# Two pieces of a cos/sin table issued on the ACT queue, and all pieces of the input back to back on the SP queue

## Chip, cores and metric

One core of one Trainium2 chip. The metric is the device time of one execution in microseconds (us). "Span" is the time from the first to the last instruction in the trace, about 1.8 us less than the device time.

The names of the engines in what follows: PE multiplies matrices; DVE, ACT and POOL work element by element; SP only issues loads. DMA is the moving of data by 16 engines of its own. A load is first issued by a queue (here that of SP or of ACT), then its packets move, and it has landed when its completion is recorded; only then may an engine that waits for it go on.

## The reference

A pre-norm layer: a spectral filter (2D real FFT, product with a complex weight, inverse FFT) on the layer-normed input, and then a gated feed-forward block.

```python
x = A_x                                              # 1 x 2048 x 576, bf16
h  = x + irfft2(rfft2(layernorm(x)) * (A_w_r + 1j * A_w_i))
h2 = h + (gelu(layernorm(h) @ B_w_gate) * (layernorm(h) @ B_w_up)) @ B_w_down
```

## The kernel before

The change touches only how the first loads are issued. The input x is loaded in five pieces (tiles 0-1, 2-3, 4-7, 8-11, 12-15 of 128 x 576; called x0 to x4), the cos/sin table ATB in three (tiles 0-3, 4-7, 8-15; called table 0, 1, 2). DVE and ACT compute row statistics of x (`bn_stats` on DVE; Identity and Square with a sum on ACT for tiles 1, 3, 7, 11, 13), the table is scaled by 1/std, and PE multiplies x by the scaled table.

```python
def x_load(i, c0, c1):
    P.dma(SP, XO[:, c0:c1, 0:D], xv[:, c0:c1, :], f"x{i}", w=[("X", c) for c in range(c0, c1)])
def atb_load(i, c0, c1):
    P.dma(SP, ATB[:, c0:c1, :], tabs[:, c0:c1, :], f"atb{i}", w=[("ATB", c) for c in range(c0, c1)])
x_load(0, 0, 2)
x_load(1, 2, 4)
atb_load(0, 0, 4)
x_load(2, 4, 8)
atb_load(1, 4, 8)
x_load(3, 8, 12)
x_load(4, 12, 16)
atb_load(2, 8, 16)
# ... cut: FT, BT, VT tables, then 36 loads of the two weight planes w_i, w_r, all on SP ...
P.op(ACT, lambda a: a.activation(SA[:, 0, 0:1], EPT[:, 0:1], ACTF.Sqrt), r=["EPT"], ...)  # dummy: brings the table load early
act_sum(1); act_sq(1)              # ACT: first use of x0
ln1_tile(0); ln1_tile(2)           # DVE: bn_stats of tile 0 (x0) and tile 2 (x1)
# ... cut: act_sum(3), variance, Sqrt, reciprocal ...
ln1_scale(0, DVE)                  # DVE: first use of table 0
# ... cut: groups 1 to 4, the same on x1 .. x4 ...
for i in range(NG):                # POOL: third weight plane = -w_i, 16 instructions
    P.op(POOL, lambda v, g=GORD[i]: v.tensor_scalar(WS[:, g, 0, :], WS[:, g, 2, :], -1.0, None, op0=ALU.mult), ...)
```

The helper makes each engine wait on semaphores for the loads and results that it reads. Each load has a semaphore of its own.

## Time and profile before

| | before |
|---|---|
| device time, median of 3 runs (lowest to highest) | 504.44 us (504.13 to 504.98) |
| span of the profiled run | 502.9 us |
| start of DVE's first instruction on x | 3.84 us |
| first matmul of the next stage (FT) | 20.33 us |

The page of the kernel before: first the line of busy time by engine, then the chain that ended last.

```profile
PE 492.4 (98%) x4318; PEld 297.7 (59%) x4319; DVE 183.9 (37%) x391; ACT 158.7 (32%) x296; POOL 39.1 (8%) x49
...
PE 91%; DVE 6%; issue 1%; DMA 1%; ACT 1%; DVEq 0%
```

PE is the engine to feed, and DMA holds 1% of the chain. That 1% is the landing of x0 (3.1 us). Of the 6% of DVE (30.5 us) 12.9 lie before 20.4 us and 17.3 between 33 and 55 us, behind all of these loads. The pieces of x and of the table are read in the first 20 us, so I read the timeline there. Its columns are start, length, engine, line, operation, written and read tiles, count, and in brackets the idle time before and what ended it. SPq is the issuing of loads by the SP queue.

```profile
0.72 1.28 ACT L517 ACT_TABLE_LOAD   x1 [0.72 <-PEq L907]
0.73 0.87 SPq L206 DMA_DIRECT2D XO<-in_A_x_dram  x2
...
1.30 0.10 POOL L378 MEMSET EPT<- 128x1 f32 x1
...
1.65 0.42 SPq L206 DMA_DIRECT2D ATB<-c_atab  x1
...
2.02 0.20 ACT L517 ACTIVATE SA<-EPT 128x1 f32<-128x1 f32 x1
2.11 0.43 SPq L206 DMA_DIRECT2D XO<-in_A_x_dram  x1
...
2.59 0.43 SPq L206 DMA_DIRECT2D ATB<-c_atab  x1
...
3.06 0.91 SPq L206 DMA_DIRECT2D XO<-in_A_x_dram  x2
...
3.84 1.55 DVE L440 BATCH_NORM_STATS2 ST<-XO 128x6 f32<-128x288 bf16 x4 [3.84 <-DMA XO<-in_A_x_dram]
...
6.44 0.42 DVE L472 TENSOR_SCALAR ATS<-ATB,RS 128x128 bf16<-128x128 bf16 x2
...
8.16 2.25 DVE L440 BATCH_NORM_STATS2 ST<-XO 128x6 f32<-128x288 bf16 x6
...
17.75 8.16 POOL L665 TENSOR_SCALAR WS<-WS 128x290 bf16<-128x290 bf16 x8 [2.05 <-DMA WS<-in_A_w_i_dram]
```

What to see: an issue takes about 0.43 us, one follows the other, and DVE waits for a load once, 3.84 us for x0. That a load is late is no cost by itself; the cost is the wait in brackets.

### The profile page before, as it was taken

The numbers are of one execution on the slowest core, as the hardware profiler recorded it, in microseconds if no ns is written. First come the engines' busy times: TensorE is split into PE (matmuls) and PEld (weight loads), VectorE is DVE, ScalarE is ACT, GpSimd is POOL, SyncE is SP. The second block draws the span as 40 slices with busy tenths as digits, with TensorE's granted clock in tenths as the row PEclk, the third lists the DMA queues.
The fourth block names the chain that finished last, engine by engine and source line by source line (L and its number), as shares of the span: only waits on it lengthen the run. The fifth ranks groups of instructions, "written<-read, shape, count | busy, mean of one in ns | idle before, by whom it ended". The sixth has DMA issues, their size and how long they took to land.

```text
span 502.9 us, 9972 instructions
## 1 busy us (share of the span) xinstructions
PE 492.4 (98%) x4318; PEld 297.7 (59%) x4319; DVE 183.9 (37%) x391; ACT 158.7 (32%) x296; POOL 39.1 (8%) x49
## 2 busy tenths in 40 slices
PE   6899999999999999999999999999999999999998
PEld 2687674444458764444477744444577644444775
DVE  5899673344431114343310134333201233333111
ACT  7888776653220003333200023323100133323000
POOL 3644281000000000000000000000000000000000
PEclk9999999999999999999999999999999999999999
DMA  8779789001100000100000001100000000000000
GB/s 284 165 224 334 235 292 353 6 4 25 25 5 13 18 19 17 22 17 1 2 7 18 19 15 23 22 4 1 1 18 19 13 1 1 1 2 2 12 19 19
DMA packets 25948, 28.64 MB, mean 57 GB/s; under 512 B 11568, under 2 KB 19888, under 8 KB 25776
## 3 DMA queue, kind: packets, MB, share of 16 engines
q1 hardware_dynamic: 23328, 17.39, 12.1%
q0 software_dynamic: 2576, 10.62, 6.3%
q8 instruction: 34, 0.56, 0.5%
q14 instruction: 10, 0.08, 0.1%
HBM read 23.66 MB, written 2.36 MB: 52 GB/s over the span
## 4 chain that ended last, share of the span: by engine, by line
PE 91%; DVE 6%; issue 1%; DMA 1%; ACT 1%; DVEq 0%
PE PS L838 56%; PE PS L861 28%; PE PS L700 3%; DVE TP L629 2%; PE PS L739 2%; PE PS L600 1%; DVE ST L440 1%; DVE CUS L606 1%; PE PS L645 1%; DVE CUS L607 1%; DMA XO<-in_A_x_dram 1%; PE PS L620 1%; DVE U L505 0%; DVE ATS L472 0%; ACT JNK L431 0%
## 5 line engine op out<-in xcount | busy, mean ns | idle before, releaser
L838 PE MATMUL PS<-HT,WGU 64*128 64x512 bf16 x2592 | 281.9, 376 | 0.0
L838 PEld LDWEIGHTS PS<-HT,WGU 64*128 64x128 bf16 x2592 | 137.3, 94 | 143.4 <-issue 1.2
L850 ACT ACTIVATE GL<-PS 128x512 bf16<-128x512 f32 x144 | 85.9, 597 | 289.3 <-PE PS L838 289.3
L851 DVE TENSOR_TENSOR AT<-GL,PS 128x512 bf16<-128x512 bf16 x144 | 99.0, 688 | 174.1 <-PE PS L838 172.5
L861 PE MATMUL PS<-WD,AT 128*128 128x288 bf16 (+2 forms) x1152 | 141.8, 286 | 0.0
L861 PEld LDWEIGHTS PS<-WD,AT 128*128 128x128 bf16 x1152 | 111.0, 98 | 31.5 <-issue 1.7
L864 DVE TENSOR_TENSOR OS<-PS,XO 128x288 bf16<-128x288 f32 (+2 forms) x32 | 14.7, 458 | 125.8 <-PE PS L861 125.8
L665 POOL TENSOR_SCALAR WS<-WS 128x290 bf16<-128x290 bf16 x16 | 15.2, 949 | 9.3 <-DMA WS<-in_A_w_i_dram 8.2
L742 DVE SCALAR_TENSOR_TENSOR XO<-PS,XO 128x576 bf16<-128x576 f32 x16 | 12.1, 756 | 8.4 <-PE PS L739 8.4
L645 PE MATMUL PS<-VT,ZS 128*128 128x256 bf16 x96 | 13.4, 272 | 1.7 <-DVE ZS L631 1.4
L600 PE MATMUL PS<-FT,U 128*128 128x290 bf16 x96 | 14.4, 287 | 0.5 <-DVE U L505 0.5
L700 PE MATMUL PS<-DT,V 128*128 128x289 bf16 x96 | 14.6, 287 | 0.2 <-DVE V L651 0.2
L629 DVE TENSOR_TENSOR TP<-YS,WS 128x580 bf16<-128x580 bf16 (+2 forms) x34 | 13.5, 438 | 0.3 <-issue 0.3
L656 ACT ACTIVATE V<-PS 128x768 bf16<-128x768 f32 x15 | 12.2, 811 | 2.1 <-PE PS L645 1.8
L623 ACT ACTIVATE YS<-PS 128x578 bf16<-128x578 f32 x16 | 10.5, 655 | 3.3 <-PE PS L620 3.3
L494 PE MATMUL PS<-ATS,XO 128*128 128x128 bf16 (+1 forms) x80 | 7.1, 223 | 4.4 <-POOL ATS L467 2.7
L709 ACT ACTIVATE GS<-PS 128x578 bf16<-128x578 f32 x15 | 9.8, 655 | 4.2 <-PE PS L700 4.1
L645 PEld LDWEIGHTS PS<-VT,ZS 128*128 128x128 bf16 x96 | 8.1, 97 | 4.8 <-DVE ZS L631 1.0
L600 PEld LDWEIGHTS PS<-FT,U 128*128 128x128 bf16 x96 | 9.2, 98 | 3.0 <-issue 0.7
L700 PEld LDWEIGHTS PS<-DT,V 128*128 128x128 bf16 x96 | 8.9, 97 | 3.4 <-DVE V L651 0.4
L730 ACT ACTIVATE OS<-XO 128x576 bf16<-128x576 bf16 x16 | 10.8, 675 | 0.0
L620 PE MATMUL PS<-CUS,BT 128*128 128x289 bf16 (+2 forms) x96 | 10.7, 247 | 0.0
(58 smaller groups left out, 158.6 us busy)
## 6 DMA issues: line engine op xcount, KB each, us to landing
WD<-in_B_w_down_dram POOLq DMA_DIRECT2D x9, 576.0 KB, 8.3
WGU<-in_B_w_up_dram SPq DMA_DIRECT2D x4, 1152.0 KB, 9.6
WGU<-in_B_w_gate_dram POOLq DMA_DIRECT2D x4, 1152.0 KB, 10.4
out_dram<-OS SPq DMA_DIRECT2D x30, 72.0 KB, 1.6
XO<-in_A_x_dram SPq DMA_DIRECT2D x3, 576.0 KB, 6.9
IT<-c_itab SPq DMA_DIRECT2D x1, 1024.0 KB, 7.0
HT<-HN SPq DMA_TRANSPOSE x60, 2.4
XO<-in_A_x_dram SPq DMA_DIRECT2D x2, 288.0 KB, 3.2
```

What stands on the lines that cost most here:

```text
L600: P.op(PE, lambda t, b=b, o=o, dt=dt, us=us, g=g: t.matmul(bank(b, 0, 128, 0, 2 * HK), U[:, us, g, :, :], FT[:, o, dt, :], start=(dt == 0) ...
L620: P.op(PE, lambda t, b=b, tb=tb, pl=pl, q0=q0, q1=q1, m=m, s3=s3, sp_=sp_: t.matmul(bank(b, 0, 128, q0, q1), BT[:, sp_, tb, :], CUS[:, s3, ...
L629: P.op(DVE, lambda v, sl=sl, g=g, q0=q0, q1=q1, t_=t_, w_=w_: v.tensor_tensor(TP[:, sl, t_, :, q0:q1], YS[:, sl, :, q0:q1], WS[:, g, w_, q ...
L645: P.op(PE, lambda t, b=b, o=o, c=c, zp=zp, sl=sl, sp_=sp_: t.matmul(bank(b, 0, 128, o, o + 256), ZS[:, sl, zp, 128 * c:128 * c + 128], VT[ ...
L656: P.op(ACT, lambda a, g=g, src=src: a.activation(V[:, :, :, g, :], src, ACTF.Copy), r=[("PS", bs[0]), ("PS", bs[2]), "Vfree"], w=[("V", g, ...
L665: P.op(POOL, lambda v, g=GORD[i]: v.tensor_scalar(WS[:, g, 0, :], WS[:, g, 2, :], -1.0, None, op0=ALU.mult), r=[k for k in wkeys[0 if 1 <= ...
L700: P.op(PE, lambda t, b=b, h=h, i=i, kt=kt, c=c: t.matmul(bank(b, 0, 128, 0, K2), V[:, kt, c, :, :], DT[:, 3 * h + i, 0:K2], start=(i == 0) ...
L838: op = P.op(PE, lambda t, h0=h0, kt=kt, wt=wt, f=f, b=b, HT=HT, s=(half == 0 and j in (0, 5)), e=(half == 1 and j in (3, 8)): t.matmul(ban ...
L850: P.op(ACT, lambda a, s2=s2, b0=b0: a.activation(GL[:, s2, :], bank(b0), ACTF.Gelu_apprx_tanh), r=[("PS", b0)], w=[("GL", s2)])
L851: P.op(DVE, lambda v, s2=s2, b0=b0, f=f: v.tensor_tensor(AT[:, f, :], GL[:, s2, :], bank(b0 + 1), op=ALU.mult), r=[("GL", s2), ("PS", b0 + ...
L861: P.op(PE, lambda t, b=b, d0=d0, d1=d1, f=f, p=p: t.matmul(bank(b, 0, 128, 0, d1 - d0), AT[:, f, 128 * p:128 * p + 128], WD[:, f, d0:d1], ...
L864: P.op(DVE, lambda v, b=b, d0=d0, d1=d1, p=p, c=c: v.tensor_tensor(OS[:, p % 2, d0:d1], bank(b, 0, 128, 0, d1 - d0), XO[:, c, d0:d1], op=A ...
```

## The change

The intent: take the two table pieces off the SP queue, so that x2 is issued one slot earlier and x3, x4 and all later loads two slots earlier, and hide the two issues on ACT, "behind its table load", where ACT waits for x0 anyway.

```diff
-    def atb_load(i, c0, c1):
-        P.dma(SP, ATB[:, c0:c1, :], ...
+    def atb_load(i, c0, c1, eng=SP):
+        P.dma(eng, ATB[:, c0:c1, :], ...
     x_load(0, 0, 2)
     x_load(1, 2, 4)
-    atb_load(0, 0, 4)
     x_load(2, 4, 8)
-    atb_load(1, 4, 8)
     x_load(3, 8, 12)
     x_load(4, 12, 16)
     atb_load(2, 8, 16)
@@
     P.op(ACT, lambda a: a.activation(SA[:, 0, 0:1], EPT[:, 0:1], ACTF.Sqrt), r=["EPT"], w=[("SA0", 0)])
+    atb_load(0, 0, 4, ACT)
+    atb_load(1, 4, 8, ACT)
     idle_mm(11, 0)
```

More of the change, by code (lines that the diff above doesn't have):

```diff
@@ L385, in x_load @@
         P.dma(SP, XO[:, c0:c1, 0:D], xv[:, c0:c1, :], f"x{i}", w=[("X", c) for c in range(c0, c1)])
-    def atb_load(i, c0, c1):
-        P.dma(SP, ATB[:, c0:c1, :], tabs[:, c0:c1, :], f"atb{i}", w=[("ATB", c) for c in range(c0, c1)])
+    def atb_load(i, c0, c1, eng=SP):
+        P.dma(eng, ATB[:, c0:c1, :], tabs[:, c0:c1, :], f"atb{i}", w=[("ATB", c) for c in range(c0, c1)])
     x_load(0, 0, 2)
     x_load(1, 2, 4)
-    atb_load(0, 0, 4)
     x_load(2, 4, 8)
-    atb_load(1, 4, 8)
     x_load(3, 8, 12)
```

## The prediction

> **What bounds the kernel.** The chain of waits puts 91% of the span on the tensor engine and only 1% on DMA. The engine table has PE busy 98%, at a granted clock of 1.000. The change touches only the first microseconds, so I read those in the timeline. The ACT table load runs 0.72 to 2.00 us, then one dummy Sqrt to 2.22, and ACT is idle until 3.84. The sync queue issues its loads back to back, about 0.46 us from one start to the next: x0 at 0.73, x1 about 1.16, table piece 0 at 1.65, x2 at 2.11, table piece 1 at 2.59, then x3, x4. Issue start plus issue-to-landing time (per-tile view) gives landings of x0 3.8, x1 4.5, table 0 4.9, x2 7.3, table 1 8.4, x3 10.0, x4 11.4 us.
>
> When is each needed? DVE waits for DMA once, 3.8 us for x0 (waits view). It starts the tile of x1 about 4.6, the tile of x2 at 8.16, that of x3 near 10.9, that of x4 near 13.7. Table 0 is first read at 6.44 (scaling), table 1 at 11.90. So x0 alone is on the chain; x1 has about 0.1 us to spare, x2 0.9, x3 0.9, x4 over 2, table 0 1.6, table 1 3.5.
>
> **What the change does.** No work is added or removed: same bytes, same descriptors. x2 moves up one issue slot (0.46 us), x3, x4 and everything later on the sync queue two (0.9 us). Two issues of about 0.43 us (estimate from the sync queue's) go to ACT at about 2.2 and 2.65, ending near 3.1; ACT's idle time to 3.84 hides them. The Trainium skill ("DMA: Bandwidth & Descriptors", Issuing engines are not separate DMA queues) says loads from different issuers run on the same 16 engines and interleave, so only issue time is saved; this trace agrees that issue is not the limit, with the DMA share near 1.0 from 5 to 17 us.
>
> **On the critical path.** The gain is nil: x0 keeps its place, and no engine waits for x2, x3 or x4. Small losses are possible. (a) Table 0, now issued 0.6 us later, has its packets (first packet about 1.2 us after issue, so near 3.4) interleave with those of x1 (3.2 to 4.3). Its 128 packets of about 46 ns on 16 engines are 0.37 us of work per engine; x1 can land up to 0.3 us later and, with 0.1 us to spare, cost up to 0.25 us. (b) Table 0 now shares with x2, and lands perhaps at 5 to 6.4 us; if it comes behind all of x2 it lands about 7 and costs 0.6 us on DVE; behind x3 too, 2 us. DVE is nearly solid from 8 to 18 us and the tensor engine waits for it at 20.3, so such a delay reaches the end. (c) The weight planes' load may arrive up to 0.9 us earlier (the POOL negation waits for it until 17.75) and shift POOL's overlap with DVE's scaling, worth 0.2 us either way.
>
> **Prediction.** 504.7 us, range 503.7 to 506.2. Faster by over 2%: 0.01; within 2%: 0.98; slower by over 2%: 0.01.
>
> **What would show it.** x2, x3, x4 land 0.3 to 1 us earlier, yet the bn_stats of tile 4 still starts at 8.2, give or take 0.4; DVE still starts at 3.84; ACT's first Identity at 3.84; a second hardware queue in the DMA table does not appear or carries 0.25 MB; first FT matmul at 20.3 within 0.5; everything after 20.3 only shifted.
>
> **What would make it wrong.** A table piece landing after 6.44 (DVE scaling then waits on DMA); an ACT issue so long that ACT's first sum starts after 3.84; x1 held up by table packets; x0 itself arriving earlier or later.

## The result

The changed kernel took 504.52 us (median of 4 runs, 504.27 to 504.84), the kernel before 504.71 us (4 runs, 504.13 to 505.09). The ratio is 0.9998, 95% interval 0.998 to 1.0015: the same. (A ratio is the mean time of one kernel's fast runs over that of the other's of the same rounds, so not quite the ratio of the medians.)

The same lines of the changed kernel's timeline; ACTq is the issuing of loads by the ACT queue.

```profile
0.72 1.28 ACT L515 ACT_TABLE_LOAD   x1 [0.72 <-PEq L907]
...
0.73 2.31 SPq L206 DMA_DIRECT2D XO<-in_A_x_dram  x5
...
1.30 0.10 POOL L378 MEMSET EPT<- 128x1 f32 x1
...
1.44 0.81 ACTq L206 DMA_DIRECT2D ATB<-c_atab  x2
...
2.01 0.20 ACT L515 ACTIVATE SA<-EPT 128x1 f32<-128x1 f32 x1
...
3.75 0.82 DVE L438 BATCH_NORM_STATS2 ST<-XO 128x6 f32<-128x288 bf16 x2 [3.75 <-DMA XO<-in_A_x_dram]
...
4.75 0.82 DVE L438 BATCH_NORM_STATS2 ST<-XO 128x6 f32<-128x288 bf16 x2 [0.17 <-DMA XO<-in_A_x_dram]
...
6.60 0.42 DVE L470 TENSOR_SCALAR ATS<-ATB,RS 128x128 bf16<-128x128 bf16 x2
...
8.31 2.25 DVE L438 BATCH_NORM_STATS2 ST<-XO 128x6 f32<-128x288 bf16 x6
...
16.03 8.19 POOL L665 TENSOR_SCALAR WS<-WS 128x290 bf16<-128x290 bf16 x8 [0.18 <-POOL ATS L465]
16.13 0.36 DVE L444 SCALAR_TENSOR_TENSOR TM<-SA 128x1 f32<-128x1 f32 x1
```

Three things to see. First, the table pieces are not issued behind the table load: the first goes out at 1.44 us, 0.04 us after POOL has written the constant that the dummy Sqrt waits for, while the table load runs until 2.00 and the Sqrt itself starts at 2.01. Second, DVE now has a second wait, for x1. The bracket says 0.17 us; but instructions of DVE that do not wait begin 0.09 us before the last one ends, so that DVE lost 0.26: tile 2 begins 1.00 us after its first instruction on x, against 0.73 before. Third, POOL's negations start 1.7 us earlier, and the DVE instruction beside their start takes 0.36 us; in the kernel before it took 0.11:

```profile
15.97 0.11 DVE L446 SCALAR_TENSOR_TENSOR TM<-SA 128x1 f32<-128x1 f32 x1
```

The page of the changed kernel, answering to the two lines shown of before, with a queue line that is new (queue, packets, MB, share of the DMA engines):

```profile
PE 493.1 (98%) x4319; PEld 299.0 (59%) x4319; DVE 183.8 (37%) x391; ACT 158.5 (32%) x296; POOL 39.2 (8%) x49
...
q10 hardware_dynamic: 288, 0.26, 0.2%
...
PE 90%; DVE 7%; issue 1%; DMA 1%; ACT 0%; SPq 0%; DVEq 0%
```

Following matched instructions through both traces, the changed kernel is 0.17 us behind at the bn_stats of tile 2, 0.16 at the last bn_stats, 0.41 at the fifth reciprocal (16.86 against 17.27) and at the first FT matmul (20.33 against 20.74), then 0.20 to 0.30 behind between 27 and 33 us, 0.18 near 36, and 0.07 from 41 us on to the end. The 0.41 is the sum of two steps: x1 (from 0.09 ahead to 0.17 behind) and the stretched instruction beside POOL (0.25). So in this pair nothing was gained in the first 20 us and 0.41 us lost, of which 0.34 came back before 41 us. (In this run of the changed kernel the granted clock of PE was 0.5 from 7.35 to 10.77 us, in the traced run of before not; between 8 and 16 us the shift of DVE stays at 0.16, so this is not where the time went.) Whether such tenths belong to the change or to the run needed repeats.

### The profile page after: what moved, and what is told of

It reads as the page before. It is cut to its first block, busy times and chain, and to the rows that moved or that the text cites. A ratio compares the mean times of both kernels' runs of the same rounds, so it can differ in the third digit from the quotient of the medians.

```text
span 503.0 us, 9973 instructions
## 1 busy us (share of the span) xinstructions
PE 493.1 (98%) x4319; PEld 299.0 (59%) x4319; DVE 183.8 (37%) x391; ACT 158.5 (32%) x296; POOL 39.2 (8%) x49
## 4 chain that ended last, share of the span: by engine, by line
PE 90%; DVE 7%; issue 1%; DMA 1%; ACT 0%; SPq 0%; DVEq 0%
PE PS L838 56%; PE PS L861 28%; PE PS L700 3%; DVE TP L629 2%; PE PS L739 2%; DVE ST L438 1%; PE PS L600 1%; DVE CUS L606 1%; DVE CUS L607 1%; DMA XO<-in_A_x_dram 1%; DVE U L503 0%; PE PS L620 0%; DVE ATS L470 0%; PE PS L645 0%; PE PS L784 0%
```

## The experiments

Theory T: after x0, DVE's own work sets the pace, so earlier x2 to x4 bring nothing; what remains is a small shift of waits (x1 beside the table packets; POOL beside DVE). Rivals: J, the shifts are jitter of single runs; G, earlier x is worth something, and x1's wait hides it. Theory F, on the two queues, came with it: loads of both queues are served in the order of their issue. Its rival, I: each queue gets its own share at once. Times are medians; the kernel before had 504.32 us in the first job (9 runs), 504.54 in the second (7) and 504.59 in the third (9); each job ran on another chip.

### Both kernels again

No edit.

> The kernel before, unchanged, as a control of how far the first 20 us move from run to run. Theory T (the change only shifts waits: x1 is held 0.17 us by the table pieces, the POOL negation starts 1.7 us earlier and collides with DVE elsewhere): the trace repeats the first one, with bn_stats of tile 2 at 4.57 us within 0.06 and no DVE wait for x1, first POOL negation at 17.75 within 0.3, first FT matmul at 20.33 within 0.1. Rival J (these differences are jitter of one run): bn_stats of tile 2 waits for x1 here too, or the negation starts anywhere between 16 and 18 us. Time 504.5 within 0.5 for both.

> The changed kernel, unchanged, as a control. Theory T: bn_stats of tile 2 again late, at 4.75 within 0.08, waiting for x1; POOL negation at 16.03 within 0.2; first FT matmul at 20.74 within 0.1; end within 0.3 us of the kernel before. Rival J: x1 no later than in the kernel before in this run, or the negation near 17.7. Ratio of the times 1.000 within 0.001.

Measured: before 504.70 us (ratio to its own other runs 1.0005, interval 0.9991 to 1.0018), changed 504.45 us (1.0001, 0.9989 to 1.0014). The landings, from the completion records of the loads in the trace, in us after the span's start:

| load | before | before again | changed | changed again | needed at, over the four runs |
|---|---|---|---|---|---|
| x0 | 3.81 | 3.50 | 3.73 | 3.62 | at once |
| x1 | 4.54 | 4.21 | 4.72 | 4.36 | 0.74 after DVE's start, 4.26 to 4.57 |
| table 0 | 4.88 | 5.96 | 5.08 | 5.51 | 6.13 to 6.60 |
| x2 | 7.29 | 7.40 | 7.06 | 7.89 | 7.84 to 8.31 |
| x3 | 9.98 | 9.63 | 8.64 | 9.28 | about 10.6 to 11.0 |
| x4 | 11.41 | 11.05 | 10.06 | 10.71 | about 13.3 to 13.8 |

Rival J is right about much. The negations began at 17.02 and not 17.75 in the kernel before, at 16.59 and not 16.03 in the changed one. The first FT matmul came at 19.80 us in the kernel before and at 20.10 in the changed one, not at 20.33 and 20.74. The changed kernel did not wait for x1 the second time. x0's landing alone moved by 0.31 us in one and the same kernel, and that shift was carried unchanged to the reciprocal near 16.7 us. x3 and x4 land earlier in both runs of the changed kernel (by 0.85 us, mean against mean), and x2 does not. Three later traces with the same order of loads (no_neg, no_neg_dve, neg_late, below) bear this out: counted from x0, x3 landed after 4.92 to 5.95 us in these five (before: 6.13 and 6.17) and x4 after 6.34 to 7.35 (before: 7.55 and 7.60), some 0.6 us earlier in the mean, x2 after 3.33 to 4.54 (before: 3.48 and 3.90). The expectations missed, for the changed kernel (a wait for x1 again, negations at 16.03) and for the kernel before (tile 2 at 4.57, negations at 17.75).

The wait for x1 can be judged by more runs. The gap between the landings of x0 and x1 was 0.73 and 0.71 us in the kernel before, 0.68 and 0.71 in two kernels below where table packets come much later, but 1.00, 0.74, 0.88, 0.90, 0.75, 1.02 and 1.12 in the seven kernels with the table pieces on ACT at 1.44 us and x1 on SP. So the table piece does hold x1 back, on average by 0.2 us, and DVE's 0.74 us on tile 0 hides a part of it or all: counted from its first instruction, DVE began tile 2 late in five of the seven traces, by 0.13 to 0.37 us, and in none of the four others. Against rival J, this shift belongs to the change; its size is jitter.

### The table pieces really behind the table load

```diff
-    def atb_load(i, c0, c1, eng=SP):
+    def atb_load(i, c0, c1, eng=SP, r=()):
-        P.dma(eng, ..., w=[...])
+        P.dma(eng, ..., r=r, w=[...])
-    atb_load(0, 0, 4, ACT)
+    atb_load(0, 0, 4, ACT, [("SA0", 0)])     # waits for the dummy Sqrt's result
```

> The changed kernel, with the first table piece made to wait for the dummy Sqrt's result, so that the two pieces are issued where the change's words put them, at about 2.25 and 2.7 us instead of 1.44 and 1.84. Theory T: the table packets come behind x2 or late in x1, so x1 is free again (bn_stats of tile 2 at 4.57 to 4.62, no wait), but if loads are served in the order of issue, table piece 0 comes behind x2 and x3's start, lands 6.5 to 9 us and the first scaling waits for it: first FT matmul at 20.7 to 22.5. Rival I (the two queues are interleaved fairly): table piece 0 lands at 5.5 to 6.4 and no engine waits; first FT matmul at 20.5. Time 504.5 to 506.5 under T, 504.5 under I.

Measured: 509.18 us, ratio 1.0087 (1.0074 to 1.0101). Lines of the timeline, the third with DVE's wait:

```profile
0.73 2.29 SPq L206 DMA_DIRECT2D XO<-in_A_x_dram  x5
2.25 0.82 ACTq L206 DMA_DIRECT2D ATB<-c_atab  x2
...
10.34 0.42 DVE L470 TENSOR_SCALAR ATS<-ATB,RS 128x128 bf16<-128x128 bf16 x2 [4.10 <-DMA ATB<-c_atab]
```

Issued 0.81 us later, table 0 landed at 10.31 us: behind x3, which had been issued at 2.11 us and landed at 9.73. Its first packet moved at 5.49 us, 3.24 us after the issue. That is not the ACT queue's own delay: where ACT's first load had nothing ahead of it, its first packet moved 1.0 to 1.15 us after the issue (the next two ACT experiments below). The rival falls. Of F the order holds: in every trace told of here the pieces of x and of the table landed in the order of their issue (but for x0 and x1 in the next ACT experiment, issued 0.01 us apart). F's sizes missed: it had table 0 landing at 6.5 to 9 us, the first FT matmul at 20.7 to 22.5 (measured 24.63) and 504.5 to 506.5 us. Nor is it one load after the other: the packets of table 0 moved between those of x3 and x4, from 5.49 to about 10 us. x1 was free, as expected (tile 2 at 4.47, no wait).

### x back to back, table pieces behind them on SP

```diff
 (kernel before)
     x_load(0, 0, 2)
     x_load(1, 2, 4)
-    atb_load(0, 0, 4)
     x_load(2, 4, 8)
-    atb_load(1, 4, 8)
     x_load(3, 8, 12)
     x_load(4, 12, 16)
+    atb_load(0, 0, 4)
+    atb_load(1, 4, 8)
     atb_load(2, 8, 16)
```

> Half of the change alone: all x pieces back to back on the SP queue, but the two table pieces behind them on the SP queue too, not on ACT. Theory F (loads of both queues are served in the order in which they were issued, so the ACT queue was worth its early issue time at 1.44 us only): table piece 0, issued last at about 2.6 us instead of 1.65, lands behind x4 at 10.5 to 12 us, DVE's first scaling waits for it and everything shifts by 4 to 5.5 us: 508.5 to 510 us. Rival S (x early is worth something by itself): x2 to x4 land earlier and the loss stays below 2 us.

Measured: 509.56 us, ratio 1.0111 (1.0091 to 1.0132). The view of waits:

```profile
DVE ATS L472 <- DMA ATB<-c_atab: 4.1, 1, 4.1
DVE ST L440 <- DMA XO<-in_A_x_dram: 3.7, 1, 3.7
```

Table 0 was issued at 3.07 us (not at 2.6, as the expectation had it), landed at 10.28 and cost DVE 4.1 us. Here x2 landed at 5.80 us, 1.5 us earlier than in the kernel before, x3 at 8.59 and x4 at 9.98, and none of it helped: DVE stood waiting for the table. So the first half of the change, alone, loses 5 us, and the early issue on ACT is what makes up for it. Rival S falls.

The rate of the loads shows why x2 gains here and not in the changed kernel. The stretch 4.25 to 5.25 us of the kernel before, the changed kernel and this one (stretch, busy time of PE, PEld, DVE, ACT and POOL, granted clock, DMA share, GB/s):

```profile
4.25:5.25 1.00, 1.00 (x5) 0.40 (x3) 1.00 (x4) 1.00 (x5) 0.24 (x1) 1.00 0.49 113
```

```profile
4.25:5.25 1.00, 0.88 (x5) 0.20 (x2) 0.82 (x3) 1.00 (x5) 0.23 (x1) 1.00 1.06 294
```

```profile
4.25:5.25 1.00, 1.00 (x4) 0.43 (x3) 1.00 (x4) 1.00 (x5) 0.23 (x1) 1.00 0.99 401
```

With a table piece between x1 and x2 the rate is low in this stretch (113 GB/s, 93 in the repeat), less so with the piece on ACT (294 GB/s, 219 in the repeat), and without one it is 401 (378 in the run behind the Sqrt). Why it falls was not tested; that the piece is the cause is argued from these runs, not shown. The changed kernel still puts table 0 between x1 (issued at 1.18) and x2 (1.65), because its ACT issue comes at 1.44: the order of service is the one of the kernel before.

### x1 on ACT, beside x0

```diff
-    def x_load(i, c0, c1):
-        P.dma(SP, ...
+    def x_load(i, c0, c1, eng=SP):
+        P.dma(eng, ...
-    x_load(1, 2, 4)
+    x_load(1, 2, 4, ACT)      # first instruction of ACT, ahead of its table load
```

> The changed kernel with x1 issued first on the ACT queue, ahead of the table load, beside x0 on the SP queue; the table pieces follow on ACT. Theory T: x1 lands at or before 4.5 us, bn_stats of tile 2 follows tile 0 without a wait, so DVE's first block ends 0.17 us earlier than in the changed kernel, if x0 itself is not slowed; with a fair interleave of x0 and x1, x0 lands 0.2 to 0.5 later and everything with it. Rival G (the earlier x2 to x4 do bring a gain, which x1's wait hides): with x1's wait gone, the first FT matmul comes 0.5 us or more before the 20.33 of the kernel before. T says not before 20.25. Time within 0.2% of the kernel before in both.

Measured: 506.82 us, ratio 1.0051 (1.0038 to 1.0065). x0, issued at 0.73, and x1, issued at 0.72, moved together (packets from 1.76 to 4.58 and from 1.87 to 4.67 us) and landed at 5.03 and 5.20. DVE started at 5.05 us, 1.21 later than in the first trace of before, and its trace ended 1.75 later. The rest is in the main a second wait, for table 0, which now came behind x2 and landed at 8.23:

```profile
8.25 0.42 DVE L470 TENSOR_SCALAR ATS<-ATB,RS 128x128 bf16<-128x128 bf16 x2 [0.71 <-DMA ATB<-c_atab]
```

T's warning came true (x0 slowed by a neighbour), but by 1.2 us and not the 0.2 to 0.5 expected, and the time left the 0.2% that both theories gave it. Rival G gets no support, though with x0 late this run could not have shown its gain.

### Table pieces on ACT before the Sqrt

```diff
-    P.op(ACT, ... Sqrt ...)
     atb_load(0, 0, 4, ACT)
     atb_load(1, 4, 8, ACT)
+    P.op(ACT, ... Sqrt ...)
```

> The changed kernel with the two table pieces issued on ACT before the dummy Sqrt (no wait for its constant), at about 0.72 and 1.1 us, so beside x0 and ahead of x1. Theory F (service by time of issue, neighbours sharing): now the table pieces hold back x0 and x1; x0 lands 0.4 to 1.0 us later than in the changed kernel, at 4.0 to 4.7, x1 at 4.9 to 5.6, DVE waits for both, and the end is 0.5 to 1.3 us later than the kernel before: 505.0 to 505.8 us. Rival I (each queue gets its own share and x0 is first on its queue): x0 lands where it did, within 0.2 us; end unchanged.

Measured: 506.29 us, ratio 1.0037 (1.0023 to 1.0050). Table 0 was issued at 0.72 us, beside x0. x0 landed at 4.76 and x1 at 5.90:

```profile
4.79 0.82 DVE L438 BATCH_NORM_STATS2 ST<-XO 128x6 f32<-128x288 bf16 x2 [4.79 <-DMA XO<-in_A_x_dram]
5.92 0.82 DVE L438 BATCH_NORM_STATS2 ST<-XO 128x6 f32<-128x288 bf16 x2 [0.31 <-DMA XO<-in_A_x_dram]
```

Each is a little beyond F's forecast, in its direction; rival I falls. Loads issued at the same moment on two queues share, and x0 pays. Together with the run behind the Sqrt this gives a window for the ACT issue: at 0.72 us it costs 1.2 us at the end of the trace and 1.7 in the medians, at 1.44 nothing that can be told from jitter, at 2.25 it costs over 4.

### How late may x2 be?

```diff
 (slack_small)                       (slack_big)
     x_load(1, 2, 4)                     x_load(1, 2, 4)
+    atb_load(2, 8, 16)             +    atb_load(2, 8, 16)
                                    +    P.dma(SP, FT..., "ft", ...)
     x_load(2, 4, 8)                     x_load(2, 4, 8)
     x_load(3, 8, 12)                    x_load(3, 8, 12)
     x_load(4, 12, 16)                   x_load(4, 12, 16)
-    atb_load(2, 8, 16)             -    atb_load(2, 8, 16)
                                    -    P.dma(SP, FT..., "ft", ...)
```

> The changed kernel, with the last table piece (0.25 MB) moved ahead of x2, so that x2, x3 and x4 are issued one slot later, as late as in the kernel before or later. Theory T (x2 to x4 have 0.3 to 2 us to spare): x2 lands 0.6 to 0.9 us later than in the changed kernel, 7.8 to 8.6, and the bn_stats of tile 4, which starts near 8.0 us anyway, moves by 0 to 0.5 us and with it the end: 504.3 to 505.1 us. Rival G (early x is worth its 0.5 to 1.3 us): the end moves by 0.7 us or more.

> As the last, with the 0.44 MB of the FT table ahead of x2 as well, so 0.7 MB more before x2. Theory T: x2 lands 1.7 to 2.2 us later than in the changed kernel, at 9 to 10 us; only now DVE waits for x2, 0.9 to 1.8 us, and the end moves by that: 505.2 to 506.4 us, ratio 1.002 to 1.004. If slack_small does not move and this one does, the slack of x2 lies between.

Measured: 504.85 us, ratio 1.0006 (0.9991 to 1.0021), and 506.28 us, 1.0034 (1.0019 to 1.0049). The bn_stats of tile 4 in each:

```profile
8.76 1.54 DVE L438 BATCH_NORM_STATS2 ST<-XO 128x6 f32<-128x288 bf16 x4 [0.43 <-DMA XO<-in_A_x_dram]
```

```profile
9.54 0.82 DVE L438 BATCH_NORM_STATS2 ST<-XO 128x6 f32<-128x288 bf16 x2 [1.14 <-DMA XO<-in_A_x_dram]
```

x2 landed at 8.73 and 9.51 us, and DVE waited 0.43 and 1.14. So DVE would have begun tile 4 near 8.3 in both, and x2 is free only until then. In the first of the two x2 was a little later than forecast, and the device time cannot tell it from the kernel before; its trace can. In the kernel before x2 came at 7.29 and 7.40, so all of it that could be brought forward was time to spare.

### What POOL's overlap costs DVE

Both of these give a WRONG RESULT ON PURPOSE (error 0.022): the negated weight plane is zeroed early instead of computed late.

```diff
-    for i in range(NG):
-        P.op(POOL, ... WS[:, g, 0, :] = -WS[:, g, 2, :] ...)
+    P.op(POOL, None, r=wkeys[1])      # only waits for the last weight loads
 (no_neg)      after POOL's other memsets:
+    P.op(POOL, lambda g: g.memset(WS[:, :, 0, 1:K2], 0.0), ...)
 (no_neg_dve)  at the start, on DVE instead:
+    P.op(DVE, lambda v: v.memset(WS[:, :, 0, 1:K2], 0.0), ...)
```

> WRONG RESULT ON PURPOSE: the changed kernel without the 16 negations of the weight plane on POOL (that plane is set to zero early instead), to size what POOL's overlap costs DVE. Theory C (each stretch of POOL work slows the DVE instructions beside it, 0.2 us at the start of the stretch and about 0.1 us per group later): first FT matmul 0.2 us earlier relative to DVE's start than in the changed kernel's first run, the DVE period of one group 1.97 instead of 2.07 us all the way, end 0.6 to 1.1 us earlier than the changed kernel: about 503.5 to 504. Rival: no overlap cost; end the same within 0.2 us of the changed kernel, once x0's landing is taken off.

> WRONG RESULT ON PURPOSE: as no_neg, but the zeroing of the plane is done by DVE in its idle time before x0 arrives, because POOL's 4 us memset of no_neg held up DVE instructions for 1.8 us and spoilt the comparison. Theory C (POOL's negations slow DVE): counted from DVE's first bn_stats, the first residual add comes 53.0 us later (53.7 to 54.05 in the two kernels' four runs), and the end is 0.6 to 1.0 us earlier than the kernel before: 503.4 to 504.0 us. Rival: no difference beyond 0.2 us.

Measured: 505.39 us (1.0017, 1.0002 to 1.0032) and 505.60 us (1.0022, 1.0009 to 1.0034). Both forecasts of the end missed, because both memsets got in the way. In the first, POOL's memset held DVE's scaling of table 0:

```profile
4.56 3.97 POOL L423 MEMSET WS<- 128x4608 bf16 x1
...
6.42 2.19 DVE L471 TENSOR_SCALAR ATS<-ATB,RS 128x128 bf16<-128x128 bf16 x2
```

The pair that takes 0.42 us elsewhere took 2.19 and ended 0.08 us after the memset. The Trainium skill ("SBUF — State Buffer", Who interferes with whom) says that DVE and GpSimd (POOL) share a port pair as an exclusive lock held for a whole instruction; this trace agrees for the scaling (0.08 us from the memset's end to its own). In the second, DVE's own memset took 3.90 us, so DVE began x only at 5.58.

Counted from a point behind these accidents, both answer. From the bn_stats of tile 15 to the first residual add it took 41.64 us in no_neg, against 42.58 and 42.66 in the kernel before and 42.50 and 42.41 in the changed one. From the first bn_stats to that add it took 53.01 in no_neg_dve (53.0 was expected), against 53.89, 53.97 and 54.05, 53.73. Up to 0.3 us of the second comparison is x1's wait, which no_neg_dve, starting late, does not have. From tile 15 on, where x1 plays no part, no_neg_dve took 41.78. So POOL's negations cost the way to the first residual add 0.6 to 1.0 us, in both kernels alike. In none of these traces does DVE wait for a result of POOL before 60 us; its instructions take longer. Whether shifting the negations takes some of that cost away is the next run.

### The negations later

```diff
-             r=[...] + ["Wz"], w=[("Wn", i)])
+             r=[...] + ["Wz"] + ([("ATS", 15)] if i == 0 else []), w=[("Wn", i)])
```

> The changed kernel, with the first POOL negation made to wait for DVE's last scaling (about 18.0 us instead of 16.0 to 16.6). Theory C: no DVE instruction between 15.5 and 18 us is stretched, so from the bn_stats of tile 10 to the first FT matmul it is 0.2 us less than in the changed kernel's first run (5.43 us there, 5.2 here); but the first stretch of negations now ends near 26.2 us and overlaps the first products, which costs the 0.2 us again. End within 0.3 us of the kernel before: 504.2 to 504.8 us. Rival: the end keeps the 0.2 us and more.

("Tile 10" in that text should read tile 15: the 5.43 us was taken from the latter.) Measured: 504.53 us, ratio 1.0002 (0.9987 to 1.0017). The negations began at 18.38 us. From the bn_stats of tile 15 to the first FT matmul it took 4.96 us, against 5.43 and 5.14 in the two runs of the changed kernel. From the first bn_stats to the first residual add it took 53.66, against 54.05 and 53.73. The kernel before had 5.19 and 4.97 to the FT matmul, so 4.96 is no more than a run of that kernel can show. The stretched DVE instructions before the FT matmul go, as expected. From tile 15 to the residual add it took 42.13, against 42.50 and 42.41: 0.3 us or so may stay, where the expectation had it paid back. One trace and a time equal to that of the kernel before cannot settle this.

## Why the prediction was right, and where it was not

- "x0 alone is on the chain" and "the gain is nil": right, shown. x0's landing shifts DVE's start one to one, x3 and x4 came earlier (by 0.85 us in the two pairs, some 0.6 over all traces) and moved nothing, x2 had 0.44 to 0.87 us to spare in the kernel before, and it took a delay past about 8.3 us to make DVE wait.
- Table issues "at about 2.2 and 2.65": wrong. They came at 1.44 and 1.81 us. The step read the program order as if ACT's issue had to wait for the table load and the Sqrt to end; it waits only for the Sqrt's semaphore. The Trainium skill ("Perfetto Trace Analysis", the part on a DVE / Act engine instruction) has the sequencer hand an instruction to a queue and go on to the next; here a load was issued 0.57 us before the Sqrt ahead of it began.
- Loss (b), table 0 late, "0.6 us" behind x2 and "2 us" behind x3: it did not happen, for the reason above. Had the issue been where the prediction put it, the run behind the Sqrt shows 4.1 us of wait, so this term was half the size of the real one. Here the prediction was lucky. Two errors cancelled: it put the issue 0.8 us too late, and it took so late an issue to be nearly free (table 0 landing at 5 to 6.4 us), where the run that issued it there measured 10.31. With its own issue time and the right landing it would have had to forecast 509.
- Loss (a), x1 held up, "up to 0.3" and costing "up to 0.25": right in kind and nearly in size. x1 came up to 0.4 us later against x0; DVE lost 0.26 us in the first run, 0 in the repeat, and 0.13 to 0.37 in four later runs.
- "x2, x3, x4 land 0.3 to 1 us earlier": right for x3 and x4 in the mean, wrong for x2, which did not come earlier. It is served behind table 0 as before, and in the stretch after x1 the DMA engines were only half busy (share 0.49 from 4.25 to 5.25 us of the kernel before), which the prediction passed over.
- (c), the negations "up to 0.9 us earlier, 0.2 us either way": the shift was 1.7 us in one pair and 0.4 in the other, the effect +0.25 us on DVE before 17 us in the first, and later returned. Right in kind and in the size of the effect, though the start of the negations moved by 0.6 to 0.7 us between two runs of one kernel.

The Trainium skill ("DMA: Bandwidth & Descriptors", Issuing engines are not separate DMA queues), on which the prediction leaned, says that a second issuer saves only the issue time. The runs agree: what the ACT queue gave was an issue at 1.44 us instead of 3.07, worth 5 us against the order of sp_only (x back to back, table pieces behind) and nothing against the order of the kernel before.

## What to carry to other kernels

Before moving a load earlier, find who waits for it and until when it would have been in time; here x2, x3 and x4, which the change meant to bring forward, had 0.4 to over 2 us to spare, and x0, the one load that was waited for, was already first. A second queue is not a second lane: in these runs what counted was the moment at which a load was issued against the loads of both queues, and 0.8 us later put a small table behind 1.2 MB of input. And compare one profile with a repeat before explaining tenths of a microsecond.

## What the Trainium skill lacked or had wrong

- "DMA: Bandwidth & Descriptors" (Queues, rings and completion order) says that each DMA engine takes turns between the queue rows that have work. That fits loads issued at the same moment (x0 and x1 on two queues, both 1.8 to 4.6 us). That section does not say that a load issued later on an idle queue can wait behind loads issued earlier on the other: table 0's first packet moved 3.24 us after its issue at 2.25 us, against 1.0 to 1.15 us with nothing ahead.
- "ScalarE: Activation LUTs" (What ACT_TABLE_LOAD costs) does not say whether the ACT queue can issue loads during a table load. It can: issued at 1.44 us, table load from 0.72 to 2.00. The page's 1283 ns for the load agrees with the 1.28 us here; its drain of about 1380 ns does not show, neither here (the Sqrt starts 0.01 us after the load) nor at a load between two busy instructions of the kernel before (107.75 to 109.03 us, 0.02 us after the one and 0.01 before the other).
- No page that I know of tells of a small piece between large ones beside which the rate of the loads falls: 113 and 93 GB/s from 4.25 to 5.25 us with the table piece there, 401 and 378 without (the cause was not tested).
- "SBUF — State Buffer" (Who interferes with whom) is right about the lock in the one case seen here; I found no figure there for a row of short POOL instructions beside DVE. Here 16 of about 0.95 us cost the way to the first residual add 0.6 to 1.0 us in all.
